# Attention and cosine router: which queue carries v and k, and when rows, constants and rank products are issued

## The chip, the cores and the metric

The kernel runs on 1 core of one Trainium2 chip. The metric is device time in microseconds (us), the median of several runs. A profile is one execution on the chip, recorded instruction by instruction.

## The reference

All arrays are float32. Attention is taken over chunks of 64 tokens, for 8 batches of 8 heads with 576 tokens of 64 numbers each; its output, regrouped to 4608 tokens of 512 numbers, goes to a router that picks one of 8 experts for each token.

```python
scores = scale * np.matmul(q_c, k_c.transpose(0, 1, 2, 4, 3))
scores = scores - np.max(scores, axis=-1, keepdims=True)
attn = np.exp(scores)
attn = attn / (np.sum(attn, axis=-1, keepdims=True) + 1e-09)
out = np.matmul(attn, v_c)
...
logits = xn @ en.T / tau
expert_idx = np.argmax(logits, axis=1)
...
    h = np.maximum(x[mask] @ w1[e], 0.0)
    out[mask] = gate_w[mask, None] * (h @ w2[e])
```

`xn` and `en` are the tokens and the expert vectors divided by their norms, and `gate_w` is the softmax probability of the expert chosen.

## The kernel before

**First stage, attention and routing.** The 4608 tokens are 36 tiles of 128 tokens (two chunks, all heads). The loop that starts at L1025 goes over t = -3 to 38 and works on several tiles at once. In step t, TensorE's order is: the weights of tile t transposed (`turn_a`), k and q of tile t+3 transposed (`turn_qk`), the scores of tile t+2 (`scores`), the attention output of tile t-1 transposed (`turn_x`), and the value products of tile t (`values`, L651). Tiles are routed in batches of four: with its last tile at t-2, `logits` multiplies by the expert vectors, `copy_logits` turns the result back, and `pick` marks each token's expert on VectorE. One step later `place` (L732) counts, with a few small products (the rank products, L737 to L746), how many tokens ahead of each one go to the same expert, and VectorE makes of this the token's row (`dest`, L765) in the DRAM array `spots`. `put` then writes one tile's rows per step to `spots` with an indirect DMA (L800). The order of instructions on each engine is the order in which the program issues them; nothing rearranges them.

**Loads.** A tile's k and q are 256 KB each (1,024 pieces of 256 bytes) and have four buffers each; `load_qk(t+7)` in step t fills the one that `turn_qk(t+3)` has just read (a tile that crosses two batches takes two loads). v is kept by batch of the input, nine chunks, in two buffers; `load_v` fills one with eight loads, one a head, of 576 pieces of 256 bytes. The first value products on v of batch b belong to tile 4.5 b, rounded down. q goes through GpSimd's DMA queue; k too, but for the first four tiles, which go through SP's; v goes through SP's queue, batch 0 in two halves before the loop, later batches after the values of a step, batch 1 in step 2.

**Constants and blank rows.** `constants` (L509) is 36 calls for GpSimd, most under 0.3 us, all issued in step 0: small tables, matrices for the rank products, and the tile `blank`. `clear_first` (L549), in step 1, writes blank rows into the first four groups of the two experts that are worked on first, and into a spare group, with three loads on SP's queue of 576, 576 and 144 KB. `values` also has GpSimd write the token numbers of each tile with an `iota` (L668) into the rows that `put` sends. The rows are a ring of eight tiles: the values of tile n+8 go where those of tile n were.

**Second stage, experts.** Tokens are read back from `spots` in groups of 64 by expert, two groups (of two experts) side by side, and multiplied by w1 and w2 (L342 and L413). The first weights are loaded in steps 28 and 30, the first groups' rows (`load_early`) from step 26 on, all through SP's queue, and the first parts of that work are issued from step 34 on (`early_parts`).

Of the kernel before, what the change touches and what calls it, by code (L numbers as in the profile page):

```python
# [18 lines left out]
P = 128  # L19
# [6 lines left out]
def kernel(  # L26
# [143 lines left out]
    def first_rows(s, j, n):  # L170
        r0 = (0, E - 1)[s] * R + G * j
        return spots[r0 : r0 + G * n, :]
# [273 lines left out]
    with (  # L446
# [59 lines left out]
        in_g = one.tile([P, 1], FP32, name="in_g")  # L506
        e_p = one.tile([P, 1], FP32, name="e_p")

        def constants():  # L509
            nc.gpsimd.iota(io_i, pattern=[[1, NST]], base=0, channel_multiplier=0)  # L510
            nc.gpsimd.iota(part_i, pattern=[[0, 1]], base=0, channel_multiplier=1)
            make_upper_triangular(nc, sltb, val=1.0, diag=False)
            nc.gpsimd.memset(onesb, 1.0)
            nc.gpsimd.memset(blank, 0.0)
            nc.gpsimd.memset(blank[:, D + TOK : D + TOK + 1].bitcast(I32), NO_ROW)
            nc.gpsimd.memset(ones, 1.0)
            nc.gpsimd.memset(before, 0.0)
            nc.gpsimd.memset(eqb_all[:, 0], 0.0)
            nc.gpsimd.memset(jump[:, 1], 1.0)
            nc.gpsimd.memset(nb[:, 0:1], float((SPARE + R) // G))  # L520
            nc.gpsimd.tensor_copy(io, io_i)
            nc.gpsimd.tensor_copy(at, part_i)
            nc.gpsimd.tensor_scalar(pref, io[:, 0:E], -1.0, float(E), ALU.mult, ALU.add)
            nc.gpsimd.tensor_scalar(e_base, io[:, 0:E], float(R), None, ALU.mult)
            nc.gpsimd.tensor_scalar(second, at, float(G), None, ALU.is_ge)
            nc.gpsimd.tensor_scalar(is_0, at, 2.0, None, ALU.is_lt)
            nc.gpsimd.tensor_scalar(lim, at, -float(P), float(G * NE), ALU.mult, ALU.add)
            nc.gpsimd.tensor_scalar(step, second, -2.0, 1.0, ALU.mult, ALU.add)
            nc.gpsimd.tensor_scalar(first_s, second, -1.0, 1.0, ALU.mult, ALU.add)
            nc.gpsimd.tensor_scalar(back, io, -1.0, float(NST - 1), ALU.mult, ALU.add)  # L530
            nc.gpsimd.tensor_scalar(more_g, back, float(LEAST - NE), None, ALU.is_ge)
            nc.gpsimd.tensor_scalar(pair_g, back, float(LEAST - NE), None, ALU.is_equal)
            nc.gpsimd.tensor_tensor(more_g, more_g, pair_g, ALU.add)
            nc.gpsimd.tensor_tensor(pair_g, back, more_g, ALU.subtract)
            nc.gpsimd.memset(more_e[:, NSW - 1 : NSW], 1)
            nc.gpsimd.tensor_scalar(e_0, second, float(E - 1), None, ALU.mult)
            nc.gpsimd.tensor_scalar(e_1, e_0, 1.0, None, ALU.add)
            nc.gpsimd.tensor_scalar(ends_e, io[:, 0:E], 0.0, None, ALU.is_equal)
            nc.gpsimd.tensor_scalar(full, io[:, 0:E], float(E - 1), None, ALU.is_equal)
            nc.gpsimd.tensor_tensor(ends_e, ends_e, full, ALU.add)  # L540
            nc.gpsimd.tensor_scalar(done, ends_e, float(NE), None, ALU.mult)
            nc.gpsimd.tensor_scalar(ends_e, ends_e, is_0, None, ALU.mult)
            nc.gpsimd.tensor_scalar(in_g, second, -float(G), at, ALU.mult, ALU.add)
            nc.gpsimd.tensor_scalar(e_p, second, float(R), None, ALU.mult)
            nc.gpsimd.tensor_scalar(
                base_h, io[:, 0 : E // 2], 2.0 * R, e_p, ALU.mult, ALU.add
            )

        def clear_first():  # L549

            for s in range(2):
                nc.sync.dma_start(
                    out=first_rows(s, 0, NE).rearrange("(j p) w -> p j w", p=G),
                    in_=blank[0:G].unsqueeze(1).to_broadcast([G, NE, W]),
                )
            nc.sync.dma_start(out=spots[SPARE : SPARE + G, :], in_=blank[0:G])

        before = one.tile([P, E], BF16, name="before")
        qk_t, qkT, v_t, st = {}, {}, {}, {}

        def load_qk(t):

            for src, nm, eng in (
                (k, "kx", nc.sync if t < 4 else nc.gpsimd),
                (q, "qx", nc.gpsimd),
            ):
                x = qk_p.tile([P, H, Dh], FP32, tag=nm, name=nm)
                done = 0
                while done < P:
                    b, s = divmod(t * P + done, S)  # L570
                    n = min(P - done, S - s)
                    eng.dma_start(  # L572
                        out=x[done : done + n],
                        in_=src[b, :, s : s + n, :].rearrange("h p d -> p h d"),
                    )
                    done += n
                qk_t[nm, t] = x.rearrange("p h d -> p (h d)")

        def load_v(b, c0=0, c1=NCB, eng=nc.sync):

            t = v_sb[b % 2]
            for h in range(H):
                r0 = CH * (h % 2)
                eng.dma_start(
                    out=t[r0 : r0 + CH, h // 2, c0:c1, 0:Dh],
                    in_=v[b, h].rearrange("(c k) d -> k c d", k=CH)[:, c0:c1],
                )
            v_t[b] = t
# [53 lines left out]
        def values(t):  # L642
            d = st[t]
            ps = ps_v.tile([P, 2, 512], FP32, tag="pv", name="pv")
            pv = ps[:, :, 0 : NPAIR * (Dh + 1)].rearrange("p r (i d) -> p r i d", d=Dh + 1)
            for i in range(NPAIR):
                for par in range(2):
                    for c in range(2):
                        b, cb = divmod(2 * t + c, NCB)
                        r0 = CH * par  # L650
                        nc.tensor.matmul(  # L651
                            pv[CH * c : CH * c + CH, par, i],
                            lhsT=d["aT"][r0 : r0 + CH, i, CH * c : CH * c + CH],
                            rhs=v_t[b][r0 : r0 + CH, i, cb, 0 : Dh + 1],
                            start=True,
                            stop=True,
                        )
            rs = wk.tile([P, 2, NPAIR], FP32, tag="rs", name="rs")
            nc.vector.tensor_scalar(rs, pv[:, :, :, Dh], 1e-9, None, ALU.add)
            nc.vector.reciprocal(rs, rs)  # L660
            x = xr[:, t % NX, 0:D]
            nc.vector.tensor_tensor(
                x.rearrange("p (i r d) -> p r i d", r=2, d=Dh),
                pv[:, :, :, 0:Dh],
                rs.unsqueeze(3).to_broadcast([P, 2, NPAIR, Dh]),
                ALU.mult,
            )
            nc.gpsimd.iota(  # L668
                xr[:, t % NX, D + TOK : D + TOK + 1].bitcast(I32),
                pattern=[[0, 1]],  # L670
                base=P * t,
                channel_multiplier=1,
            )
            st[t] = {"x": x}

        def turn_x(t):
# [31 lines left out]
        def copy_logits(b):  # L708
            n, t = sizes[b], sum(sizes[:b])
            nc.tensor.transpose(lt_ps, copied[b], ident)  # L710
            copied[b] = xr[:, t % NX : t % NX + n, D : D + E]
            nc.vector.tensor_copy(
                copied[b], lt_ps.rearrange("p (n e) -> p n e", e=Q)[:, 0:n, 0:E]
            )
# [278 lines left out]
        load_qk(1)  # L993
        for x in v_sb:
            nc.vector.memset(x[:, :, :, Dh : Dh + 1], 1.0)
        load_qk(2)
        load_qk(3)
        load_v(0, 0, 4)
        load_v(0, 4, NCB)
        norm_experts()  # L1000
        nc.gpsimd.memset(xr[:, :, D:W], 0.0)

# [18 lines left out]

        early_t = 26
        ends = {sum(sizes[: b + 1]) - 1: b for b in range(len(sizes))}
        for t in range(-3, NT + 3):

            if 0 <= t < NT:
# [3 lines left out]
            if t + 3 < NT:  # L1030
                turn_qk(t + 3)
                if t + 7 < NT:
                    load_qk(t + 7)
            if t - 2 in ends:
                logits(ends[t - 2])
            if t == NT:
# [3 lines left out]
                scores(t + 2)  # L1040
            if t - 2 in ends:
                copy_logits(ends[t - 2])
            if t - 3 in ends:
                place(ends[t - 3])
            if 0 <= t - 1 < NT - 1:
                turn_x(t - 1)
            if 0 <= t < NT:
                values(t)
                b = (2 * t + 2) // NCB + 1
                if b not in v_t and b < B and t > 1:  # L1050
                    load_v(b)
            if t == NT - 8:
                load_first(w1_sb, w1_rows)
            if t == NT - 6:
# [14 lines left out]
            early_parts(t, 1)  # L1069
            if t == -2:  # L1070
                turn_experts()
            if t == 0:
                constants()
            if t == 1:
                clear_first()
        groups()
        pad_places()
        put(len(to_put))
# [148 lines left out]
```

## Time and profile before

| What | us |
|---|---|
| median of 3 runs (673.04 to 680.07) | 674.3 |
| the profiled execution, and its span | 673.1, 671.3 |
| TensorE matmul busy | 623.0 (93%) |
| ScalarE busy | 443.8 (66%) |
| VectorE busy | 421.3 (63%) |
| GpSimd busy | 155.3 (23%) |
| value products of tile 0 and of tile 35 begin | 15.54, 162.11 |

In the lines of a profile PE is TensorE's matmuls, PEld its weight loads, DVE VectorE, ACT ScalarE, POOL GpSimd and SP the engine that issues most DMAs; a `q` behind an engine means its instruction queue. L651 is line 651 of the kernel before. A timeline row has the start, the length, engine, line, operation, what is written and read, the shape and how many instructions are merged; in brackets stand the idle time of the engine before it and what ended that. A busy line has one digit for each fortieth of the span, in tenths. In the DMA part, q0 is GpSimd's queue and q1 SP's: packets, MB moved, and their time as a share of 16 DMA engines. Instructions that only issue a DMA from GpSimd count as busy there.

### The profile page before, as it was taken

The page shows a single profiled execution, that of the slowest core. Times are in us where ns is not written, and L with a number is a line of the kernel's source. Part 1 is how long each engine was busy: PE and PEld are TensorE (multiplying, and loading weights), DVE is VectorE, ACT ScalarE, POOL GpSimd, SP SyncE. Part 2 cuts the span into 40 slices and gives each one's busy share as a digit, 9 for nine tenths or more (in the row PEclk, how much of TensorE's full clock was granted, in tenths as well). Part 3 has the DMA queues.
Part 4 walks back from the last instruction along what each step waited for, and adds up shares of the span by engine and source line. Part 5 has one row for each costly group of instructions (what it writes and reads, how often), then busy time and mean ns, then how long its engine had stood idle before and what let it go on. Part 6 is the DMA issues. An engine that isn't in the chain of part 4 may idle for free. (4 is left out here: it accounts for less than half of the span.)

```text
span 671.3 us, 24844 instructions
## 1 busy us (share of the span) xinstructions
PE 623.0 (93%) x9744; PEld 346.2 (52%) x9744; DVE 421.3 (63%) x1140; ACT 443.8 (66%) x776; POOL 155.3 (23%) x237
## 2 busy tenths in 40 slices
PE   6869998998898989999999999999999999999993
PEld 5658787885443446666434444334444444444431
DVE  4738888986598536547675566757655666565430
ACT  5627776775225847777777867778777677877740
POOL 8827787843310100010000100010001000100101
PEclk9969999999999989999999999999999999999997
DMA  9978999989818711113786111777811115411111
GB/s 256 275 180 233 275 288 269 275 246 371 330 55 300 285 45 35 50 34 111 290 305 210 50 42 43 290 274 253 327 52 50 38 47 167 166 43 34 50 31 35
DMA packets 94590, 112.66 MB, mean 168 GB/s; under 512 B 52364, under 2 KB 72588, under 8 KB 94456
## 3 DMA queue, kind: packets, MB, share of 16 engines
q1 hardware_dynamic: 82728, 72.84, 34.1%
q0 software_dynamic: 11696, 38.04, 17.0%
q8 instruction: 81, 1.33, 0.8%
q14 instruction: 53, 0.43, 0.2%
q10 hardware_dynamic: 32, 0.02, 0.0%
HBM read 334.71 MB, written 22.69 MB: 532 GB/s over the span
## 5 line engine op out<-in xcount | busy, mean ns | idle before, releaser
L413 PE MATMUL y_ps<-w,hT 128*32 128x512 f32 (+1 forms) x2368 | 273.2, 589 | 3.1 <-DVEq L299 3.1
L361 ACT ACTIVATE h<-C 64x256 f32<-64x256 f32 x264 | 178.6, 676 | 95.5 <-DVE C L374 68.9
L413 PEld LDWEIGHTS y_ps<-w,hT 128*32 128x32 f32 x2368 | 93.2, 110 | 153.6 <-issue 123.8
L428 POOL DMA_INDIRECT out_dram<-y,spot x36 | 34.9, 968 | 437.0 <-ACT C L377 198.0
L374 DVE TENSOR_TENSOR C<-C,h 128x256 f32<-128x256 f32 x231 | 96.1, 416 | 49.2 <-DVEq L299 42.5
L342 PE MATMUL h<-w,S 128*32 128x256 f32 x1056 | 98.1, 379 | 1.8 <-DVE w L291 1.8
L342 PE MATMUL h<-sums,xbT 128*32 128x256 f32 x1056 | 97.0, 379 | 0.0
L342 PE MATMUL h<-w,xbT 128*32 128x256 f32 x1056 | 79.4, 380 | 7.0 <-ACTq L299 5.8
L368 DVE STREAM_TRANSPOSE hT<-h 128x512 f32<-128x512 f32 x66 | 46.7, 708 | 44.1 <-ACT h L361 44.0
L342 PEld LDWEIGHTS h<-w,xbT 128*32 128x32 f32 x1056 | 40.8, 110 | 43.2 <-ACTq L299 13.5
L342 PEld LDWEIGHTS h<-w,S 128*32 128x32 f32 x1056 | 49.2, 110 | 24.4 <-DVE w L291 1.5
L342 PEld LDWEIGHTS h<-sums,xbT 128*32 128x32 f32 x1056 | 48.9, 110 | 21.9 <-ACT C L377 0.4
L227 DVE TENSOR_SCALAR rn<-rn 128x1 f32<-128x1 f32 x37 | 5.7, 153 | 72.1 <-ACT rn L224 72.1
L342 PE MATMUL h<-sums,S 128*32 128x256 f32 x528 | 48.7, 379 | 0.0
L800 POOL DMA_INDIRECT spots<-xr,dest x36 | 37.1, 1029 | 35.0 <-DVE dest L765 10.1
L203 DVE STREAM_TRANSPOSE xbT<-xin 128x256 f32<-128x256 f32 x73 | 44.4, 646 | 0.5 <-DVE hT L368 0.5
L224 ACT ACT_TABLE_LOAD x34 | 43.6, 1283 | 0.9 <-issue 0.4
L421 ACT ACTIVATE y<-y_ps,gate 128x512 f32<-128x512 f32 (+1 forms) x37 | 25.2, 682 | 28.6 <-issue 14.7
L231 ACT ACT_TABLE_LOAD x34 | 43.6, 1283 | 0.6
L682 ACT COPY xT<-tr 128x512 f32<-128x512 f32 x36 | 21.1, 586 | 34.2 <-PE tr L680 34.2
L651 PE MATMUL pv<-v,aT 64*64 64x65 f32 x1152 | 28.1, 226 | 9.0 <-DMA v<-in_v_dram 7.4
L572 POOL DMA_DIRECT2D kx<-in_k_dram x36 | 31.5, 876 | 16.4 <-PE tr L595 16.1
(202 smaller groups left out, 800.4 us busy)
## 6 DMA issues: line engine op xcount, KB each, us to landing
w<-in_moe_w_dram SPq DMA_DIRECT2D x74, 2048.0 KB
next_w<-in_moe_w_dram SPq DMA_DIRECT2D x67, 2048.0 KB
xin<-spots SPq DMA_DIRECT2D x158, 64.0 KB
qx<-in_q_dram POOLq DMA_DIRECT2D x32, 256.0 KB, 7.7
v<-in_v_dram SPq DMA_DIRECT2D x56, 144.0 KB
kx<-in_k_dram POOLq DMA_DIRECT2D x28, 256.0 KB, 5.7
spot<-spots SPq DMA_DIRECT2D x80, 4.0 KB
spots<-blank SPq DMA_DIRECT2D x2, 576.0 KB
```

Of the source, the lines that this page charges most:

```text
L203: nc.vector.transpose(xT[:, :, cols].rearrange("p c (b i) -> p b c i", i=Q), t[:, s * (D // 2) : (s + 1) * (D // 2)].rearrange("p (b i c) ...
L224: nc.scalar.activation(rn, spot[:, j % SPOTS, SQ : SQ + 1], AF.Sqrt)
L231: nc.scalar.activation(sh, sh, AF.Exp, accum_out=gate)
L342: nc.tensor.matmul(ps[t0 : t0 + Q], lhsT=a[:, c, s], rhs=w[:, r], start=c == 0, stop=c == KD // 2 - 1,)
L361: nc.scalar.activation(h[b][G * v : G * v + G, s].rearrange("p (k i) -> p k i", i=Q), x[G * s : G * s + G].rearrange("p (i k) -> p k i", i=Q),
L368: nc.vector.transpose(hT.rearrange("p k (s b i) -> p b s k i", b=2, i=Q)[:, b], h[b].rearrange("p s (k i) -> p s k i", i=Q),)
L374: nc.vector.tensor_tensor(out, a, b, op)
L413: nc.tensor.matmul(ps[Q * r : Q * r + Q, 0:w], lhsT=d["hT"][:, c, Q * t0 : Q * t0 + Q], rhs=w2_sb[s][buf_of(j)][:, c, d0 : d0 + w], start= ...
L428: ins = nc.gpsimd.indirect_dma_start(out=to, out_offset=bass.IndirectOffsetOnAxis(ap=at, axis=0), in_=y[:, 0:w], in_offset=None, bounds_ch ...
L572: eng.dma_start(out=x[done : done + n], in_=src[b, :, s : s + n, :].rearrange("h p d -> p h d"),)
L651: nc.tensor.matmul(pv[CH * c : CH * c + CH, par, i], lhsT=d["aT"][r0 : r0 + CH, i, CH * c : CH * c + CH], rhs=v_t[b][r0 : r0 + CH, i, cb, ...
L800: ins = nc.gpsimd.indirect_dma_start(out=spots, out_offset=bass.IndirectOffsetOnAxis(ap=at, axis=0), in_=m, in_offset=None, bounds_check=S ...
```

## The change

- v goes through GpSimd's queue and k of all tiles through SP's. Only the first four chunks of batch 0's v stay on SP's queue.
- Before the loop, SP issues k of tiles 0 and 1, then the first four chunks of v, then k of tiles 2 and 3. The other five chunks are issued in steps -2 and -1, four heads each. v of batch b is issued in two steps, four heads each, the first being the step t in which 2t/9 + 1, rounded down, reaches b (steps 0 and 1 for batch 1, 5 and 6 for batch 2), ahead of the step's other work and behind its k and q.
- `constants` becomes a generator of 15 parts, one a step from step 0 on, with `blank` in the first; `clear_first` becomes nine DMAs of 144 KB, two a step from step 1 on.
- The token numbers of four tiles are written by one `iota` in `copy_logits`, instead of one a tile in `values`.
- `place` comes behind `values` in its step, so the rank products follow the value products on TensorE and the row arithmetic follows the normalized values on VectorE.

```diff
-        def constants():
+        def constant_parts():
             nc.gpsimd.iota(io_i, pattern=[[1, NST]], base=0, channel_multiplier=0)
             nc.gpsimd.iota(part_i, pattern=[[0, 1]], base=0, channel_multiplier=1)
+            nc.gpsimd.memset(blank, 0.0)
+            nc.gpsimd.memset(blank[:, D + TOK : D + TOK + 1].bitcast(I32), NO_ROW)
+            yield
             make_upper_triangular(nc, sltb, val=1.0, diag=False)
             nc.gpsimd.memset(onesb, 1.0)
...
         def clear_first():
 
-            for s in range(2):
-                nc.sync.dma_start(
-                    out=first_rows(s, 0, NE).rearrange("(j p) w -> p j w", p=G),
-                    in_=blank[0:G].unsqueeze(1).to_broadcast([G, NE, W]),
-                )
+            for j in range(NE):
+                for s in range(2):
+                    nc.sync.dma_start(out=first_rows(s, j, 1), in_=blank[0:G])
+                    yield
             nc.sync.dma_start(out=spots[SPARE : SPARE + G, :], in_=blank[0:G])
...
-                (k, "kx", nc.sync if t < 4 else nc.gpsimd),
+                (k, "kx", nc.sync),
                 (q, "qx", nc.gpsimd),
...
-        def load_v(b, c0=0, c1=NCB, eng=nc.sync):
+        def load_v(b, c0=0, c1=NCB, heads=range(H), eng=nc.gpsimd):
 
             t = v_sb[b % 2]
-            for h in range(H):
+            for h in heads:
...
-            nc.gpsimd.iota(
-                xr[:, t % NX, D + TOK : D + TOK + 1].bitcast(I32),
-                pattern=[[0, 1]],
-                base=P * t,
-                channel_multiplier=1,
-            )
             st[t] = {"x": x}
...
             nc.tensor.transpose(lt_ps, copied[b], ident)
+            nc.gpsimd.iota(
+                xr[:, t % NX : t % NX + n, D + TOK].bitcast(I32),
+                pattern=[[P, n]],
+                base=P * t,
+                channel_multiplier=1,
+            )
...
+        load_v(0, 0, 4, eng=nc.sync)
         load_qk(2)
         load_qk(3)
-        load_v(0, 0, 4)
-        load_v(0, 4, NCB)
...
+            if t in (-2, -1):
+                load_v(0, 4, NCB, range(4 * (t + 2), 4 * (t + 2) + 4))
+            b = 2 * t // NCB + 1
+            if t >= 0 and b < B and v_half.get(b, 0) < 2:
+                m = v_half[b] = v_half.get(b, 0) + 1
+                load_v(b, heads=range(4 * m - 4, 4 * m))
...
-            if t - 3 in ends:
-                place(ends[t - 3])
             if 0 <= t - 1 < NT - 1:
                 turn_x(t - 1)
             if 0 <= t < NT:
                 values(t)
-                b = (2 * t + 2) // NCB + 1
-                if b not in v_t and b < B and t > 1:
-                    load_v(b)
+            if t - 3 in ends:
+                place(ends[t - 3])
...
-            if t == 0:
-                constants()
-            if t == 1:
-                clear_first()
+            if t >= 0:
+                next(constants, None)
+            if t >= 1:
+                next(clears, None)
+                next(clears, None)
```

More of the change, by code (lines that the diff above doesn't have):

```diff
@@ L507 @@
         e_p = one.tile([P, 1], FP32, name="e_p")
-        def constants():
+        def constant_parts():
             nc.gpsimd.iota(io_i, pattern=[[1, NST]], base=0, channel_multiplier=0)
             nc.gpsimd.iota(part_i, pattern=[[0, 1]], base=0, channel_multiplier=1)
+            nc.gpsimd.memset(blank, 0.0)
+            nc.gpsimd.memset(blank[:, D + TOK : D + TOK + 1].bitcast(I32), NO_ROW)
+            yield
             make_upper_triangular(nc, sltb, val=1.0, diag=False)
             nc.gpsimd.memset(onesb, 1.0)
-            nc.gpsimd.memset(blank, 0.0)
-            nc.gpsimd.memset(blank[:, D + TOK : D + TOK + 1].bitcast(I32), NO_ROW)
-            nc.gpsimd.memset(ones, 1.0)
+            nc.gpsimd.tensor_copy(io, io_i)
+            nc.gpsimd.tensor_copy(at, part_i)
+            yield
+            nc.gpsimd.tensor_scalar(pref, io[:, 0:E], -1.0, float(E), ALU.mult, ALU.add)
+            nc.gpsimd.tensor_scalar(e_base, io[:, 0:E], float(R), None, ALU.mult)
@@ L517, in constants @@
             nc.gpsimd.memset(before, 0.0)
             nc.gpsimd.memset(eqb_all[:, 0], 0.0)
+            nc.gpsimd.memset(ones, 1.0)
+            yield
             nc.gpsimd.memset(jump[:, 1], 1.0)
             nc.gpsimd.memset(nb[:, 0:1], float((SPARE + R) // G))
[L521 to L524, printed above, removed]
+            yield
@@ L525, in constants @@
             nc.gpsimd.tensor_scalar(second, at, float(G), None, ALU.is_ge)
             nc.gpsimd.tensor_scalar(is_0, at, 2.0, None, ALU.is_lt)
+            yield
             nc.gpsimd.tensor_scalar(lim, at, -float(P), float(G * NE), ALU.mult, ALU.add)
             nc.gpsimd.tensor_scalar(step, second, -2.0, 1.0, ALU.mult, ALU.add)
+            yield
             nc.gpsimd.tensor_scalar(first_s, second, -1.0, 1.0, ALU.mult, ALU.add)
             nc.gpsimd.tensor_scalar(back, io, -1.0, float(NST - 1), ALU.mult, ALU.add)
+            yield
@@ L531, in constants @@
             nc.gpsimd.tensor_scalar(more_g, back, float(LEAST - NE), None, ALU.is_ge)
             nc.gpsimd.tensor_scalar(pair_g, back, float(LEAST - NE), None, ALU.is_equal)
+            yield
             nc.gpsimd.tensor_tensor(more_g, more_g, pair_g, ALU.add)
             nc.gpsimd.tensor_tensor(pair_g, back, more_g, ALU.subtract)
+            yield
             nc.gpsimd.memset(more_e[:, NSW - 1 : NSW], 1)
             nc.gpsimd.tensor_scalar(e_0, second, float(E - 1), None, ALU.mult)
+            yield
@@ L537, in constants @@
             nc.gpsimd.tensor_scalar(e_1, e_0, 1.0, None, ALU.add)
             nc.gpsimd.tensor_scalar(ends_e, io[:, 0:E], 0.0, None, ALU.is_equal)
+            yield
             nc.gpsimd.tensor_scalar(full, io[:, 0:E], float(E - 1), None, ALU.is_equal)
             nc.gpsimd.tensor_tensor(ends_e, ends_e, full, ALU.add)
+            yield
             nc.gpsimd.tensor_scalar(done, ends_e, float(NE), None, ALU.mult)
             nc.gpsimd.tensor_scalar(ends_e, ends_e, is_0, None, ALU.mult)
+            yield
@@ L543, in constants @@
             nc.gpsimd.tensor_scalar(in_g, second, -float(G), at, ALU.mult, ALU.add)
             nc.gpsimd.tensor_scalar(e_p, second, float(R), None, ALU.mult)
+            yield
             nc.gpsimd.tensor_scalar(
@@ L549, in clear_first @@
         def clear_first():
-            for s in range(2):
-                nc.sync.dma_start(
-                    out=first_rows(s, 0, NE).rearrange("(j p) w -> p j w", p=G),
-                    in_=blank[0:G].unsqueeze(1).to_broadcast([G, NE, W]),
-                )
+            for j in range(NE):
+                for s in range(2):
+                    nc.sync.dma_start(out=first_rows(s, j, 1), in_=blank[0:G])
+                    yield
             nc.sync.dma_start(out=spots[SPARE : SPARE + G, :], in_=blank[0:G])
         before = one.tile([P, E], BF16, name="before")
-        qk_t, qkT, v_t, st = {}, {}, {}, {}
+        qk_t, qkT, v_t, st, v_half = {}, {}, {}, {}, {}
         def load_qk(t):
             for src, nm, eng in (
-                (k, "kx", nc.sync if t < 4 else nc.gpsimd),
+                (k, "kx", nc.sync),
                 (q, "qx", nc.gpsimd),
@@ L1023 @@
         ends = {sum(sizes[: b + 1]) - 1: b for b in range(len(sizes))}
+        constants, clears = constant_parts(), clear_first()
         for t in range(-3, NT + 3):
```

## The prediction

> **What bounds the kernel now.** I read the page first: its slices show TensorE (PE) nearly full except in slices 2 to 4, and its granted clock falling to 6 tenths in slice 3. Then the timeline of PE there, the busy time by stretches, the timelines of SP and GpSimd (POOL), the DMA queues in short stretches, and the waits.
>
> ```profile
> PE   6869998998898989999999999999999999999993
> PEclk9969999999999989999999999999999999999997
> ```
>
> ```profile
> 30.20 0.44 PE L651 MATMUL pv<-v,aT 64*64 64x65 f32 x10
> ...
> 32.38 0.33 PE L651 MATMUL pv<-v,aT 64*64 64x65 f32 x4 [1.03 <-DMA v<-in_v_dram]
> 38.29 0.93 PE L651 MATMUL pv<-v,aT 64*64 64x65 f32 x8 [5.58 <-DMA v<-in_v_dram]
> ...
> 46.17 0.69 PE L651 MATMUL pv<-v,aT 64*64 64x65 f32 x32
> ```
>
> The second fence is PE's timeline (start, length, engine, line, and in brackets the idle time before). Tile 4 is the first tile that needs v of batch 1. Its value products begin at 30.20 and those of tile 5 at 46.17: 15.97 us, where the same pair of steps later (tile 8 at 56.94, tile 9 at 61.36) takes 4.42. The hole costs 15.97 - 4.42 = 11.55 us: about 9.5 of waiting (the products end at 40.44 instead of 30.9), and 2 because PE then runs at half clock:
>
> ```profile
> 35.00:40.00 5.00, 1.44 (x13) 0.91 (x13) 0.00 (x0) 0.00 (x0) 0.00 (x0) 0.50 0.83 205
> 40.00:45.00 5.00, 5.00 (x54) 4.20 (x58) 1.75 (x4) 1.18 (x3) 1.92 (x3) 0.54 0.87 197
> 45.00:50.00 5.00, 4.61 (x122) 3.95 (x118) 4.01 (x13) 2.95 (x7) 1.81 (x3) 1.00 0.34 107
> 50.00:55.00 5.00, 4.73 (x120) 4.12 (x120) 4.76 (x14) 3.95 (x10) 3.41 (x6) 1.00 0.45 144
> ```
>
> (The last three columns are clock, DMA share and GB/s.) Why v is late stands in SP's and POOL's timelines:
>
> ```profile
> 17.64 2.34 SPq L552 DMA_DIRECT2D spots<-blank  x2
> 20.02 1.43 SPq L556 DMA_DIRECT2D spots<-blank  x1
> 21.50 38.91 SPq L584 DMA_DIRECT2D v<-in_v_dram  x20
> ```
>
> ```profile
> 15.04 0.88 POOL L572 DMA_DIRECT2D qx<-in_q_dram  x1
> ...
> 24.78 1.00 POOL L572 DMA_DIRECT2D kx<-in_k_dram  x1 [0.21 <-issue]
> ```
>
> SP sends 1.3 MB of blank rows first, and these had to wait for POOL's constants; POOL itself issues no load from 15.9 to 24.8. From 20 to 25 us SP's queue (q1) moved 1.36 MB and POOL's (q0) 0.02. Once both are loaded, from 15 to 20, it reads:
>
> ```profile
> q0 software_dynamic: 303, 1.00, 66.7%
> q1 hardware_dynamic: 1898, 0.46, 44.7%
> ```
>
> So q1, in packets of 256 B, gets about 0.1 MB/us and q0, in packets of 3.3 KB, 0.2. That is why 1.2 MB of v took until 39.
>
> From tile 5 to 30 PE sets the pace: 3.90 us a tile, (143.68 - 46.17)/25, with waits of only some 5 us in all, while DMA runs at 281 GB/s (share 1.00 from 60 to 140). What follows goes by tile numbers, not by times, so a gain at tile 4 reaches the end.
>
> **The change part by part.** The profiled execution is 673.1 us, its span 671.3; the median of the runs, 674.3, is 1.2 above it.
>
> *A. The hole.* Removed by issuing v(1) at tiles 0 and 1, ahead of the blank rows, and in the queue that gets 0.2 MB/us: up to -11.55. What is late next is D.
>
> *B. The rank products behind the values.*
>
> ```profile
> PE rt_ps L737 <- DVE eqb_all L728: 5.5, 9, 1.8
> ```
>
> Seven of these waits are 0.33 to 0.40, one is 1.83 (157.60), and the last, 1.40 (174.44), has no values left to be put ahead of it. In the seven batches the next tile also waits 0.27 for the normalized values, which DVE now writes ahead of the place arithmetic (four instructions, 0.8 us). At most 7 x 0.65 + 1.8 = 6.4, at least 0, if DVE, 68.7 busy of 80 us, has no room; no less, since PE's order only puts ready work ahead of a wait and the later place arithmetic is counted in E. At 157 the wait covered the copies that the next products need, so I take half, 0.9, and 0.37 a batch: 2.6 + 0.9 = -3.5.
>
> *C. The start.* SP now sends eight v loads (0.52 MB) ahead of k of tiles 2 and 3. k of tile 2 ends after 1.31 MB of q1; that queue moved 0.54 MB by 5 us and 0.56 by 10, so it lands near 12.2. PE turned it at 10.80: +1.4. Tile 3 comes at 14.6 and is asked for at 13.27, the same delay. Bounds 0 (GpSimd's queue is emptier now, q1 faster) to 3.
>
> *D. v(1) in its new place.* A v load has 576 pieces of 256 B. POOL issues a k or q load of 1,024 pieces in 0.89 us and one of 512 in 0.69 (two in 1.39), so I take 0.72. From its q load at 7.55, POOL has five tiles of q (4.9), 16 loads of v (11.3, the 5-chunk ones overpriced) and one part of constants (1.0): the last v(1) load goes out near 24.7. It lands 4.1 to 7.7 later (medians of k and q), at 28.8 to 32.4; the products ask for it at 30.2 + 1.4 = 31.6. +0.5, bounds 0 and 3.
>
> *E. The puts.* POOL issues in order. In a tile with half a batch of v it now has q 0.89, four v loads 2.9, the put 1.03 and parts of constants (0.4 to 0.6 a tile): 5.3 us in a 3.9 us tile, twice in 4.5 tiles. Compiled, each POOL load also waits until the one eight before it has landed. The put of tile n must land before DVE writes the values of tile n+8 into the same rows: in the trace the first put of a batch starts at 52.67, takes 4.0 to 5.4 to land, and the write starts at 58.44: 0.4 to 1.8 spare. Four v loads (0.59 MB) ahead of it in its queue take 2.9 us at 0.2 MB/us, half of it already gone when the put is issued; the place arithmetic comes some 0.3 later. That leaves about 0.75 of stall, in the four batches (tiles 6, 10, 14, 18) whose first put shares a tile with v: +3.0. Bounds 0 and 6 x 3 = 18, a full stall for each of the six later batches of v.
>
> *F. At nothing.* 36 counts become 9 (27 x 0.15 off POOL, which has idle time to hide it). k on q1 replaces v on q1: 0.26 MB a tile either way, four tiles ahead of use (15 us), 2.6 us of that queue. Near the end k of tiles 34 and 35 stands behind SP's early row loads, which wait for puts; three tiles of lead cover some 4 us of that, and if they did not, each would cost its delay. The blank rows now pass between k loads, done before the first put at tile 6.
>
> Sum: -11.55 - 3.5 + 1.4 + 0.5 + 3.0 = -10.15; span 661.2, execution 663.0, and 1.2 for the median: **664 us**.
>
> One rule speaks against the change. The Trainium skill (DMA: Bandwidth & Descriptors, "Issuing engines are not separate DMA queues") says that loads from any engine share the same 16 DMA engines and that another issuer saves only issue time. The trace agrees on the sum (297 GB/s from 15 to 20 us, like either queue's best) but not that the issuer is indifferent: 1.00 MB against 0.46 in the same 5 us. By the rule alone A would be only the blank rows' 1.3 MB, 4.7 us at 280 GB/s, and the time about 671.
>
> **The rivals.**
>
> *R1, slower: GpSimd's queue becomes the bound.* Per batch of v (4.5 tiles, 17.5 us) it issues q 4.5, puts 4.6, v 5.8, counts 0.2: 15.1, and 17.5 loads with eight in flight. That holds while a load lands within 17.5 x 8/17.5 = 8 us; q's median is 7.7 now. At 9.3 a cycle takes 20.3, +2.8 x 6 cycles = 17 in place of E's 3.0: span 675, time 678; it is slower than before once landing passes 9.0 (13.2/6 = 2.2 a cycle, 19.7 x 8/17.5). For it: the closeness of 7.7 to 8. Against it: v loads are smaller than q's (144 KB against 256), and k's leave the queue.
>
> *R2, the transfers fill the hole.* Between 35 and 60 us the DMA engines were idle for (0.17 + 0.13 + 0.66 + 0.55 + 0.26) x 5 = 8.9 us. If the 281 GB/s of the steady stage are all they give, no more than that comes back, and B is lost: 671.3 - 8.9 + 1.4 + 3.0 = 666.8, time 670. For it: share 1.00. Against it: 297 and 313 GB/s in the stretches at 15 and 5 us.
>
> *R3, the hole stays in part*, because POOL's loads of v(1) wait for each other at the start: half of A lost, +5.8, time 670.
>
> **How the numbers follow.** About 1% is what a measurement can tell here. Main case 0.57; R2 0.20; R3 0.08; R1 0.10; better than the main case (C, D, E all 0, B full: 671.3 - 18 = 653.3, time 656) 0.05. The likeliest case's own range is 658 to 668. The range reaches over R2 and R3 and part of R1: 657 to 675. Faster by over 1% means below 667.6: most of the main case, the better one and a fifth of R2 and R3, 0.66; slower means above 681, the worse half of R1, 0.06; the rest 0.28.
>
> **What would show it.** A: no wait for v above 1 us at tile 4, the clock at 1.00 from 35 to 45, and tile 5's values near 35 instead of 46. B: waits at the rank products below 0.2. C: a wait for k near 11 to 15 us. E: the normalized values' write waiting for puts; R1: POOL over 95% busy or waiting on its own loads from 60 to 140, with the tile above 3.9 us. R2: DMA share over 1.0 throughout and PE waiting for q, k or v. I am wrong if v through POOL lands later than 9 us after issue, or if a tile comes out slower than 3.9 us.

## The result, and the profile after

| | before | after |
|---|---|---|
| median (20 runs each, same chip) | 676.2 us | 680.82 us |
| profiled execution, span | 673.1, 671.3 us | 681.7, 679.8 us |
| value products of tile 0 / 4 / 5 begin | 15.54 / 30.20 / 46.17 | 18.94 / 32.28 / 40.31 |
| of tile 33 / 35 | 154.49 / 162.11 | 161.29 / 168.20 |

The ratio is 1.0067 [1.0044, 1.0089]: no gain, and on this chip a small loss. On two other chips, where the kernel before took 687.0 and 686.7 us, the same change measured 0.9982 [0.9959, 1.0005] and 1.0015 [0.9983, 1.0047]. The change is worth nothing within a measurement's reach; the 10 us forecast are missing on all three.

The medians differ by 4.6 us, the two profiled executions by 8.5: that of before is one of the fastest of its 20 runs (672.65 to 682.08), that of after lies 0.9 above its median. So the split that follows holds for this pair of executions and overstates the typical loss. The tile starts split the 8.5 us between the two spans: tile 4 is late by 2.08; the hole between tiles 4 and 5 shrinks from 15.97 to 8.03 (-7.94); from tile 5 to tile 33 the kernel takes 120.98 instead of 108.32 (+12.66); tiles 33 to 35 give -0.71; what follows tile 35 takes 511.6 instead of 509.2 (+2.4). Their sum is 8.49.

The page's busy lines, after:

```profile
PE   5999888888898989999999999999999999999991
POOL 7869886753321000000000100010010001001000
PEclk9989989989999999999999999999999999999997
```

The gap in slices 2 and 3 is gone, but slices 5 to 10, mostly nines before, are now all eights: the loss is spread. POOL shows 6 to 9 in its first eight slices.

PE's timeline at the start, before:

```profile
8.36 1.09 PE L595 MATMUL tr<-ident,qx 128*128 128x128 f32 x4 [0.26 <-DMA qx<-in_q_dram]
...
10.80 0.66 PE L595 MATMUL tr<-ident,kx 128*128 128x128 f32 x4
11.29 0.60 PE L595 MATMUL tr<-ident,qx 128*128 128x128 f32 x4
```

And after, at the start and at the old hole:

```profile
7.98 1.06 PE L608 MATMUL tr<-ident,qx 128*128 128x128 f32 x4
...
12.95 1.09 PE L608 MATMUL tr<-ident,kx 128*128 128x128 f32 x4 [2.32 <-DMA kx<-in_k_dram]
...
16.80 1.06 PE L608 MATMUL tr<-ident,kx 128*128 128x128 f32 x4
...
20.45 0.60 PE L608 MATMUL tr<-ident,qx 128*128 128x128 f32 x4
...
34.42 0.57 PE L664 MATMUL pv<-v,aT 64*64 64x65 f32 x20 [1.69 <-issue]
...
40.31 0.70 PE L664 MATMUL pv<-v,aT 64*64 64x65 f32 x32
```

k of tile 2 is 2.32 us late. In both kernels four transposes take about 1.06 us at first. In before they take 0.60 to 0.66 from 10.80 on, as soon as tile 2 comes; in after they still take 1.06 to 1.09 when tile 2 comes, and 0.60 only some 5 us later. At tile 4 a wait of 1.69 remains (the view names no releaser; that it is for v is read from the loads' times below), and behind it TensorE runs at a lower granted clock, as the busy times by stretches show (the busy times of PE, PEld, DVE, ACT and POOL, then clock, DMA share and GB/s):

```profile
35.00:40.00 5.00, 5.00 (x79) 4.32 (x80) 2.00 (x5) 1.44 (x3) 2.21 (x3) 0.66 0.87 254
40.00:45.00 5.00, 5.00 (x127) 4.29 (x126) 4.58 (x14) 3.90 (x9) 4.39 (x10) 1.00 0.74 204
```

The waits from 0 to 225 us, after (total, times, longest):

```profile
DVE xr L675 <- DMA spots<-xr,dest: 20.0, 14, 3.2
PE tr L687 <- DVE lmax L737: 7.7, 6, 2.6
...
POOL spots L813 <- issue: 5.0, 19, 0.3
...
PE rt_ps L750 <- DVE eqb_all L741: 1.4, 1, 1.4
```

The last row answers to the 5.5 us in nine waits of before: one is left, the batch that has no values to hide behind. The first row is new: VectorE's write of the normalized values waits for puts 14 times. In before, the only waits for puts were those of GpSimd's `iota`, 11.7 us in seven, and no wait of VectorE. Behind it TensorE waits for what VectorE does next (second row). GpSimd's timeline shows why the puts are late:

```profile
78.12 2.99 POOL L597 DMA_DIRECT2D v<-in_v_dram  x4
81.41 1.09 POOL L813 DMA_INDIRECT spots<-xr,dest  x1 [0.30 <-issue]
82.59 0.27 POOL L559 TENSOR_SCALAR base_h<-io,e_p 128x4 f32<-128x4 f32 x1
82.81 1.46 POOL L585 DMA_DIRECT2D qx<-in_q_dram  x2
84.25 2.97 POOL L597 DMA_DIRECT2D v<-in_v_dram  x4
87.53 1.07 POOL L813 DMA_INDIRECT spots<-xr,dest  x1 [0.30 <-ACT lq L710]
```

From 78.12 to 88.60 GpSimd issues without a pause, apart from 0.30 us ahead of each put. The put at 87.53 stands behind two half batches of v. The put at 81.41 is tile 8's and that at 87.53 tile 9's; VectorE waits for them with the values of tiles 16 and 17, eight tiles on in the ring (VectorE's timeline):

```profile
86.95 0.69 DVE L675 TENSOR_TENSOR xr<-pv,rs 128x512 f32<-128x512 f32 x1 [1.67 <-DMA spots<-xr,dest]
92.22 0.69 DVE L675 TENSOR_TENSOR xr<-pv,rs 128x512 f32<-128x512 f32 x1 [2.18 <-DMA spots<-xr,dest]
```

It does not look like the transfers: a put lands 5.0 us after its issue, where before took 4.9 (medians), q's landing fell from 7.7 us to 5.2, and from 45 to 145 us the DMA engines moved 249 GB/s where before moved 260. The page's DMA issues, after (KB each, us to landing):

```profile
qx<-in_q_dram POOLq DMA_DIRECT2D x32, 256.0 KB, 5.2
v<-in_v_dram POOLq DMA_DIRECT2D x56, 144.0 KB, 5.0
```

### The profile page after: what moved, and what is told of

It reads as the page before. It is cut to its first block, busy times and chain, and to the rows that moved or that the text cites. A ratio compares the mean times of both kernels' runs of the same rounds, so it can differ in the third digit from the quotient of the medians.

```text
span 679.8 us, 24806 instructions
## 1 busy us (share of the span) xinstructions
PE 624.4 (92%) x9744; PEld 337.3 (50%) x9744; DVE 419.7 (62%) x1140; ACT 446.0 (66%) x776; POOL 169.9 (25%) x238
## 3 DMA queue, kind: packets, MB, share of 16 engines
q0 software_dynamic: 13040, 38.57, 17.2%
## 5 line engine op out<-in xcount | busy, mean ns | idle before, releaser
L413 PE MATMUL y_ps<-w,hT 128*32 128x512 f32 (+1 forms) x2368 | 273.1, 586 | 3.1 <-DMA w<-in_moe_w_dram 2.9
L413 PEld LDWEIGHTS y_ps<-w,hT 128*32 128x32 f32 x2368 | 85.5, 110 | 161.3 <-issue 146.4
L342 PE MATMUL h<-w,S 128*32 128x256 f32 x1056 | 100.6, 379 | 1.8 <-DVE w L291 1.8
L342 PE MATMUL h<-sums,xbT 128*32 128x256 f32 x1056 | 99.3, 379 | 0.0
L597 POOL DMA_DIRECT2D v<-in_v_dram x64 | 47.1, 765 | 0.4 <-issue 0.4
L421 ACT ACTIVATE y<-y_ps,gate 128x512 f32<-128x512 f32 (+1 forms) x37 | 25.2, 682 | 26.7 <-issue 13.4
L585 POOL DMA_DIRECT2D qx<-in_q_dram x40 | 36.0, 902 | 11.1 <-PE tr L608 9.8
```

Source lines behind the costliest of these rows:

```text
L342: nc.tensor.matmul(ps[t0 : t0 + Q], lhsT=a[:, c, s], rhs=w[:, r], start=c == 0, stop=c == KD // 2 - 1,)
L413: nc.tensor.matmul(ps[Q * r : Q * r + Q, 0:w], lhsT=d["hT"][:, c, Q * t0 : Q * t0 + Q], rhs=w2_sb[s][buf_of(j)][:, c, d0 : d0 + w], start= ...
L585: eng.dma_start(out=x[done : done + n], in_=src[b, :, s : s + n, :].rearrange("h p d -> p h d"),)
L597: eng.dma_start(out=t[r0 : r0 + CH, h // 2, c0:c1, 0:Dh], in_=v[b, h].rearrange("(c k) d -> k c d", k=CH)[:, c0:c1],)
```

## The experiments

Theory: GpSimd's own time for issuing is what the change uses up. v on its queue makes puts late, and VectorE and TensorE wait for them. Rivals: the transfers themselves (bytes in GpSimd's queue, or the sum of DMA) are what is late; or the order alone, v ahead of the put, and not the amount; or something else in the change, such as the rank products' new place. Each ratio is to runs of the kernel before on the same chip. e_rank, e_queues_back, e_half and e_dummy shared one chip, c_before, c_after, e_put_first and e_best a second, c_after2, e_start, e_best2 and e_best3 a third. Tile starts and waits (VectorE's, for puts) are those of one profiled execution each.

The changed kernel itself did not run on the first of these chips. The two clearest comparisons are of kernels on one chip with one edit between them: e_dummy against e_queues_back, and e_best2 against e_start.

| Kernel | median, us | ratio to before | puts waited for, us (times) | tile 5, tile 35 begin |
|---|---|---|---|---|
| e_rank | 683.6 | 0.9960 [0.9929, 0.9991] | 6.7 (6) | 46.0, 168.3 |
| e_queues_back | 680.75 | 0.9937 [0.9901, 0.9973] | 5.6 (3) | 38.5, 166.9 |
| e_half | 679.37 | 0.9909 [0.9876, 0.9943] | 4.8 (5) | 37.7, 164.4 |
| e_dummy | 687.05 | 1.0008 [0.9971, 1.0045] | 9.4 (8) | 37.7, 173.8 |
| c_before | 687.03 | 1.0010 [0.9983, 1.0036] | 0.8 (1) | 48.0, 174.0 |
| c_after | 686.18 | 0.9982 [0.9959, 1.0005] | 13.4 (10) | 38.9, 166.3 |
| e_put_first | 684.94 | 0.9983 [0.9962, 1.0005] | 8.4 (8) | 39.0, 166.9 |
| e_best | 696.65 | 1.0153 [1.0124, 1.0183] | 8.7 (6) | 35.7, 184.1 |
| c_after2 | 688.57 | 1.0015 [0.9983, 1.0047] | 11.4 (8) | 42.5, 170.4 |
| e_start | 684.95 | 0.9994 [0.9961, 1.0027] | 14.3 (9) | 36.4, 166.2 |
| e_best2 | 678.95 | 0.9893 [0.9856, 0.9930] | 5.7 (5) | 36.4, 163.7 |
| e_best3 | 683.43 | 0.9952 [0.9924, 0.9981] | 8.7 (6) | 38.7, 165.9 |

### e_rank: the rank products alone

The kernel before, with `place` behind `values`:

```diff
-            if t - 3 in ends:
-                place(ends[t - 3])
             if 0 <= t - 1 < NT - 1:
...
                     load_v(b)
+            if t - 3 in ends:
+                place(ends[t - 3])
```

> The kernel before, with the one edit that the rank products stand behind the values. Theory 1 (GpSimd's issue time is what made the changed kernel slow; the rank edit is a small gain of its own): ratio to before 0.995 (my step B, -3.5 us of 676), the waits of TensorE for the picked experts from 5.5 to about 2 us, no write of normalized values waiting for a put. Rival (the later place arithmetic by itself makes the puts late): ratio 1.00 to 1.01, with waits for puts of 5 us and more.

The ratio is worth 0.4% or 2.7 us (the medians differ by 2.1), beside the 3.5 of term B. The rank products' waits fall to 1.4 us. It is not this part that loses the time. But the expectation that no write waits for a put failed: VectorE waits 6.7 us for puts even without v on GpSimd's queue, as the rival had it, though without the loss that the rival expected.

### e_queues_back: all of the change but the queues

```diff
-                (k, "kx", nc.sync),
+                (k, "kx", nc.sync if t < 4 else nc.gpsimd),
...
-        def load_v(b, c0=0, c1=NCB, heads=range(H), eng=nc.gpsimd):
+        def load_v(b, c0=0, c1=NCB, heads=range(H), eng=nc.sync):
```

> The changed kernel, with only the queues put back: v on SP's queue, k from tile 4 on GpSimd's. Everything else of the change stays. Theory 1 (v on GpSimd costs 64 issues of 0.77 us in order ahead of the puts): the 12 us lost between tiles 13 and 33 do not arise, waits for puts under 3 us in all, ratio to before 0.985 to 0.99. Rival 2 (the hole at tile 4 closed because v went into the queue that gets 0.2 MB/us): v of batch 1 is late again on SP's queue, a hole of 5 us or more at tile 4, ratio 0.995 to 1.0.

v is back on SP's queue, and the hole stays closed. PE's timeline of e_queues_back, at the start of the value products of tiles 4 and 5:

```profile
33.54 0.45 PE L664 MATMUL pv<-v,aT 64*64 64x65 f32 x12
34.17 0.56 PE L664 MATMUL pv<-v,aT 64*64 64x65 f32 x20 [0.18 <-issue]
38.45 0.68 PE L664 MATMUL pv<-v,aT 64*64 64x65 f32 x26
```

The two starts are 4.9 us apart, where c_before on another chip has 17.4 and after 8.0. So what fills the hole is the order of SP's loads and blank rows, with v(1) first. GpSimd's larger share of the DMA engines isn't needed for it. The Trainium skill (DMA: Bandwidth & Descriptors, "Issuing engines are not separate DMA queues") says that the issuing engine saves only issue time; in this place the runs agree with it, and not with my argument of 1.00 against 0.46 MB. Rival R2 falls as well: at 297 GB/s from 35 to 40 us the transfers passed without a hole.

The theory's own forecasts for this kernel were missed. Puts are waited for 5.6 us and not under 3, the ratio is 0.9937 and not 0.985 to 0.99 (nor 0.995 to 1.0, as the rival had it). And tiles 13 to 33, where the 12 us were not to arise, take 86.6 us here; they take 77.6 in before's first profile, 83.5 in c_before's on another chip, and 89.7 in after. A long loop thus stands even where no v passes through GpSimd. One chip against another is a weak comparison, but what these profiles don't show is that GpSimd's issuing makes the whole 12 us.

### e_half: half of each batch of v on either queue

```diff
-                load_v(b, heads=range(4 * m - 4, 4 * m))
+                load_v(b, heads=range(4 * m - 4, 4 * m), eng=nc.gpsimd if m == 1 else nc.sync)
```

> The changed kernel, with the second four heads of each later batch of v on SP's queue: GpSimd issues 32 loads of v less 4, a dose of half. Theory 1: GpSimd has 3.1 us less per 4.5 tiles, the waits for puts fall from 20 us to 5 or less, ratio to before 0.99. Rival 3 (the puts are late because they land late, behind other bytes in GpSimd's queue): the queue still holds q and half of v, waits for puts of 10 us, ratio 0.998.

With four v loads of each later batch off GpSimd, the waits of VectorE for puts fall to 4.8 us in five. GpSimd's groups of after, 40 to 150 us (busy, mean ns, idle time before):

```profile
L597 POOL DMA_DIRECT2D v<-in_v_dram x47 | 35.1, 779 | 0.4 <-issue 0.4
L813 POOL DMA_INDIRECT spots<-xr,dest x24 | 25.4, 1058 | 15.5 <-ACT xT L689 9.0 <-issue 2.4 <-DVE qxT L613 1.2
L585 POOL DMA_DIRECT2D qx<-in_q_dram x26 | 23.4, 903 | 1.5 <-PE tr L608 0.6 <-issue 0.5 <-PE tr L687 0.2
```

Two of these groups of e_half:

```profile
L813 POOL DMA_INDIRECT spots<-xr,dest x28 | 29.1, 1041 | 31.3 <-ACT xT L689 14.9 <-DVE before L784 5.5 <-DMA v<-in_v_dram 3.5
L597 POOL DMA_DIRECT2D v<-in_v_dram x20 | 14.9, 774 | 0.0
```

One load costs the same; there are 20 instead of 47 in that window, and the idle time ahead of puts doubles from 15.5 to 31.3. Ahead of puts, GpSimd now waits more for its data. The edit is worth nothing that the times can tell against e_queues_back on the same chip (679.37 and 680.75); what half of v is worth against all of it is read from e_best2 and e_start below.

### e_dummy: issue time without transfers

e_queues_back, and in the two steps of each later batch GpSimd clears 2048 numbers a partition of a buffer that nothing uses yet. This is work added; no byte is transferred by it.

```diff
                 load_v(b, heads=range(4 * m - 4, 4 * m))
+                nc.gpsimd.memset(w2_sb[0][0][:, 0:4], 0.0)
```

> As the kernel with only the queues put back, but in the two steps in which a batch of v is issued GpSimd also clears 2048 numbers of a buffer that nobody uses yet, about 2.1 us, so that in these steps its time is that of the changed kernel while its queue carries no v. Theory 1 (issue time): the waits for puts come back, 10 us or more, and the time is 8 to 15 us above the kernel with only the queues put back. Rival 3 (bytes in the queue): no waits for puts, the same time within 2 us.

GpSimd's clears in e_dummy, 40 to 150 us:

```profile
L1053 POOL MEMSET w<- 128x2048 f32 x11 | 20.2, 1834 | 0.0
```

Eleven clears of 1.83 us are in the window. The time rises by 6.3 us over e_queues_back (687.05 against 680.75, the intervals just touch at 0.997), tiles 5 to 35 take 136.1 us instead of 128.4, and puts are waited for 9.4 us instead of 5.6. The means of 12 runs each differ by 5.8 us, with an interval of 3.7 to 8.0 by their scatter. GpSimd being busy in these steps is enough to cost time, with the transfers left where they were. I had expected 10 us of waits and 8 us or more in the time; both are a bit less. The size is not that of the change: with k's loads on its queue too, GpSimd is busy for 88.5 of the 100 us from 45 to 145 here, and for 82.6 in after.

### c_before and c_after: both kernels again

Unchanged copies of the two.

> The kernel before, unchanged, so that its profile stands beside those of this call: ratio 1.00 within 0.3%. Both theories: no more than 2 us of waits for puts.

> The changed kernel, unchanged, for the same reason: ratio 1.005 to 1.01, 15 to 25 us of waits for puts.

Here the two are alike (0.9982), where I expected 1.005 to 1.01 and 15 to 25 us of waits for puts; there were 13.4. The difference to the first chip lies in the kernel before: from tile 5 to tile 35 the change takes 127.9 us in the first profile, 127.5 here and 128.0 on the third of these chips, but before takes 115.9 in the first and 126.1 here. Its rank products wait longer here, and GpSimd's `iota` waits somewhat longer for puts (the waits of c_before):

```profile
POOL xr L668 <- DMA spots<-xr,dest: 15.4, 5, 6.1
PE rt_ps L737 <- DVE eqb_all L728: 9.5, 9, 3.2
```

Before had 5.5 at the rank products and 11.7 at the `iota` in its first profile. These rows don't make up 10 us, so why its loop is slower here stays open. The gain is lost elsewhere on this chip: from c_before to c_after tile 4 begins 1.0 us earlier, the hole shrinks by 8.1, tiles 5 to 35 take 1.4 us longer, and what follows tile 35 takes 515.0 instead of 509.3 (+5.7); the spans differ by 2.0. The 12.66 us in tiles 5 to 33 hold for the first pair of profiles only.

### e_put_first: v behind the put of its step

```diff
-            b = 2 * t // NCB + 1
-            if t >= 0 and b < B and v_half.get(b, 0) < 2:
...
             put(1 if t < NT - 2 else 2)
+            b = 2 * t // NCB + 1
+            if t >= 0 and b < B and v_half.get(b, 0) < 2:
```

> The changed kernel, with the loads of a half batch of v issued behind the put of their step instead of ahead of it. GpSimd issues exactly the same. If its issue time as a whole is short (GpSimd over 95% busy from tile 9 to 20), the lateness only moves to the next put: waits for puts fall by less than half, from 20 us to 11 or more, ratio to before 1.00. If only the order inside a step matters, they fall under 5 us, ratio 0.99.

The waits for puts fall from 13.4 to 8.4 us, the time does not (0.9983, as c_after). Order alone gains nothing; the amount that GpSimd issues is the same, and the next put is late instead. It also warns against adding up the put waits as lost time: 5 us of them went and no time came back.

### e_start: k of tiles 2 and 3 ahead of the first v

```diff
-        load_v(0, 0, 4, eng=nc.sync)
         load_qk(2)
         load_qk(3)
+        load_v(0, 0, 4, eng=nc.sync)
```

> The changed kernel again, as the control for the other three on the same chip. Expected: 1.00 of the kernel before, give or take 0.007, value products of tile 0 beginning at 16 to 19 us, puts waited for 13 to 20 us in all by tile 36.

> The changed kernel with one thing moved: k of tiles 2 and 3 goes ahead of the first four chunks of v on SP's queue, as in the kernel before. If the late start comes from k standing behind v (my term C), the value products of tile 0 begin at 15.2 to 16.0 us, no wait for k above 1 us is left, and the time is 1 to 3 us below the changed kernel's, about 0.3% . The rival: the first v is late instead, and tile 0's products wait for v by about what k gained, no change in time. Either way tiles 13 to 33 go on losing time to GpSimd's issuing, so what is gained at the start may be lost by tile 33, since the late puts then wait for less: in that case tile 0 is 1 to 3 us earlier and tile 33 is not.

The start is as in the kernel before: tile 0 begins at 15.32 instead of 19.01 in c_after2, and the transposes of tile 2 take 0.60 to 0.66 with no wait. That settles the cause of the late start: the 3.4 us of after (3.7 here) come from k behind v on SP's queue. Tile 5 is 6.1 us earlier than in c_after2 and tile 35 is 4.2 earlier; the medians differ by 3.6 us, but the two intervals overlap, so the gain at the end is not shown by the times.

### e_best, e_best3 and e_best2: a better version

e_best joins e_put_first, e_half and e_start. e_best3 is e_best with the last half batch of v back on GpSimd's queue:

```diff
-                load_v(b, heads=range(4 * m - 4, 4 * m), eng=nc.gpsimd if m == 1 else nc.sync)
+                load_v(b, heads=range(4 * m - 4, 4 * m), eng=nc.sync if m == 2 and b < B - 1 else nc.gpsimd)
```

e_best2 is e_half and e_start only.

> Half of each later batch of v on SP's queue, both halves issued behind the put of their step, and k of tiles 2 and 3 issued ahead of the first chunks of v again. If GpSimd's issue time explains the late puts and the order of SP's first loads explains the late start (3.4 us at tile 0), the ratio to before is 0.98 to 0.985: the half batches alone gave 0.991, the start adds 3 us, the put order 1 to 2. Rival: v of batch 1, now later by most of a step, opens the hole at tile 4 again, ratio 0.99 to 0.995.

> The version in which v is issued behind the put of its step, half of it on SP, and k of tiles 2 and 3 ahead of the first v (1.0153, with one wait of 17.9 us for the last half batch of v behind the row and weight loads on SP's queue), with that one half batch put back on GpSimd's queue. If that wait was the whole of its loss, it goes to 0.987 to 0.993 of the kernel before, with no wait for v above 2 us. If the loss was elsewhere, it stays above 1.00.

> The changed kernel with the second half of each later batch of v on SP's queue (where the half-and-half kernel of the first set was 0.991 of the kernel before) and k of tiles 2 and 3 ahead of the first v. If both causes add up, 0.985 to 0.990 of the kernel before: value products of tile 0 at 15.2 to 16.0, of tile 5 at 35 to 37, of tile 29 at 133 to 139, waits for puts 3 to 8 us. If the start is hidden behind GpSimd's issuing later on, 0.991 as without it. If SP's queue, with k, v halves and rows, is late, a wait for v above 3 us shows at one batch.

e_best missed by one wait, `pv` for v of 17.9 us at tile 31. SP's timeline of e_best:

```profile
143.74 3.53 SPq L128 DMA_DIRECT2D w<-in_moe_w_dram  x2
147.37 5.18 SPq L153 DMA_DIRECT2D xin<-spots  x2
...
162.84 2.69 SPq L597 DMA_DIRECT2D v<-in_v_dram  x4
```

v of the last batch is issued in step 28 behind the put, and so behind the first expert weights and row loads. In e_half the same load goes out ahead of them. With it on GpSimd's queue (e_best3) the wait is gone and the ratio 0.9952, 2.0% less: that load was most of the loss, though 0.987 to 0.993 was expected. e_best2 beats both kernels at 0.9893 [0.9856, 0.9930]; e_half without the start's edit had 0.9909 [0.9876, 0.9943], so the start adds nothing that these times can tell.

e_best2 differs from e_start by the half batches alone, on the same chip: 678.95 against 684.95 us, with the slowest of its six runs (681.79) below the fastest of e_start's twelve (682.08). Waits for puts fall from 14.3 to 5.7 us. So half of v taken off GpSimd's queue is worth 6.0 us. With e_dummy, where GpSimd's time grew and the transfers did not, this is the evidence for issue time. It is worth 6 us, not 12.

## Why the prediction was wrong

The failed step is E, and with it the condition put on R1. The sentence "so a gain at tile 4 reaches the end" failed with it: in the first pair of profiles after is 5.9 us ahead at tile 5 and 8.5 behind at the end, in the second (c_before, c_after) 9.1 ahead and then only 2.0.

*E, +3.0.* Tiles 5 to 33 were forecast at -0.5 (B and E together) and measured at +12.66 in the first pair of profiles. On the chip of c_before and c_after tiles 5 to 35 lost 1.4 us, since before was slower there. The prediction had the right pieces: "5.3 us in a 3.9 us tile, twice in 4.5 tiles". It then priced only the bytes ahead of the put in its queue ("take 2.9 us at 0.2 MB/us, half of it already gone"), and found 0.75 us of stall. The backlog of GpSimd itself was left out: two such steps in a row put it 2 x (5.3 - 3.9) = 2.8 us behind, against 0.4 to 1.8 to spare. By that estimate a stall is 1.0 to 2.4 us. In VectorE's timeline eight of the 14 are between 1.25 and 2.2, the longest 3.19, and they come in pairs, one for each of the batches 3 to 7 of v (70 and 75 us, 87 and 92, 104 and 109, 126 and 131, 146 and 151), not once in four batches. e_dummy shows that GpSimd's time alone can have this effect (+6.3 us), and e_best2 against e_start that half of v less gains 6.0. That the backlog makes all of the 12.66 isn't shown: e_queues_back has a loop as long. The bounds, 0 and 18, held the loss; the value taken did not.

*R1 tied to the wrong number.* It was to decide "once landing passes 9.0" us. Landing fell to 5.0 and 5.2, so by that test R1 was dead, and yet GpSimd came near to being the bound in places, by issuing: it is busy for 92% of the time from 75 to 95 us, though only 70% from 100 to 120, and R1's other sign, over 95% from 60 to 140, was not met (81%). Its cycle was put at 15.1 us of 17.5. By the rows of after it is q 4.4 (23.4 us beside 24 puts in the window, x 4.5), puts 4.5 x (1.058 + 0.26) = 5.9 (the 0.26 from 5.0 us in 19 waits), v 8 x 0.779 = 6.2, counts 0.2: 16.7, and in the first 14 tiles parts of the constants on top. The misses are the idle time ahead of each put (1.2 a cycle), and 0.72 instead of 0.78 for a v load (0.5). With 0.8 us spare in 17.5, a backlog of 2.8 would hardly be worked off before the next. The other sign of being wrong did show: tiles came out at 4.20 us from 5 to 29 ((141.14 - 40.31)/24).

*C, +1.4, was 3.4.* k of tile 2 came at 12.95, beside 12.2 forecast. The rest is that TensorE, which needs nearly twice the time for each instruction at the start of both kernels, did so until after 17 us in after and only until 10.8 in before. The prediction had no term for that. e_start confirms the mechanism: without the wait for k the transposes take 0.60 to 0.66 from 10.55 on. The bounds, 0 and 3, did not hold it.

*D, +0.5, was 3.6* (8.03 - 4.42): a wait of 1.69, and behind it the clock of 0.66. The last v(1) loads were to go out near 24.7; they went out from 24.95 to 27.88. The issue time was right, 17.2 us from the q load at 7.6; on top came 3.0 us in which GpSimd waited for TensorE to free q's buffers (0.33, 2.27 and 0.41), the longest of them behind C's late k. C and D were added as if they were independent. They are one chain.

*A and B were right in kind.* The hole is closed where D isn't late (4.9 us between the starts in e_queues_back), but by order and not by GpSimd's share. B alone is worth 2.7 of the 3.5. R3, loads of v that wait for each other, hardly shows: in after no load of GpSimd waits for another at the start, in c_after one does, for 0.95 us.

*Not foreseen at all:* what follows tile 35 takes 2.4 us longer in after than in before; it is 511.5 to 517.1 in the versions with the change in them and 513.4 in e_rank, 509.2 and 509.3 in the two profiles of before. TensorE's waits don't explain it: one of 2.9 us for weights at L413 has its like in before (3.1). No experiment was aimed at it, so its cause is open. Open too is how the loss in tiles 5 to 35 splits between puts and the rest, and why before's own loop differs by 10 us between two profiles on two chips.

## What to carry to other kernels

When DMAs move to an engine that issues in order, add up its issue time for each step, not only for the cycle, carry the backlog from one step to the next, and compare it with what the latest dependent of that queue has to spare. Before crediting a queue for a gain, ask whether the order alone gives it: here it did, and dividing v between two queues, in the new order, was worth 0.9% (e_half) and 1.1% (e_best2) where moving all of it was worth nothing. Profile the kernel before on the same chip as the one after, and more than once: here its own loop took 115.9 and 126.1 us in two profiles, a difference as large as the effect. A load that is last of its kind must not be put behind the first loads of the next stage on an in-order queue.

## What the runs showed of the hardware

- A load of 576 pieces of 256 bytes cost GpSimd 0.78 us to issue (47 in the window). At the 281 GB/s of the steady stage its 144 KB take about 0.52 us (144 x 1024 / 281,000). The issue is the longer of the two, though it is short beside the 5.0 us from issue to landing. The Trainium skill says in the section named above that the issue "is usually small relative to the DMA itself": that agrees with the trace for one load by itself, and not for a row of such loads, where GpSimd's 0.78 us add up and the landings overlap.
- An indirect put of 128 rows cost 1.06 us, and GpSimd mostly stood idle 0.16 to 0.30 us ahead of it even where nothing was waited for (5.0 us in 19 such waits).
- At the start of both kernels TensorE took 1.06 to 1.13 us for each group of four transposes or 32 score products, and 0.60 to 0.69 later on. The change came at 10.8 us in before, and after 17 us in after, where a wait of 2.32 us came between. The clock column reads 1.00 from 9 to 13 us in before and from 9 to 21 us in after, so that only the durations show it.
- At tile 4 of after a wait of 1.69 us was followed by four transposes of 1.06 us again, and there the clock column does show it (0.66 from 35 to 40 us).
